# A gated feed-forward layer: gate and up by Strassen's seven block products, and down in eight-bank groups with streamed weights

## The chip, the cores and the metric

The kernel runs on one core of one Trainium2 chip. The metric is the device time of one execution in microseconds (us). The clock named below is the TensorE clock that the profile calls granted. PE is TensorE's matmul side, PEld its weight loads, DVE the vector engine, ACT the scalar engine, POOL the GpSimd engine, SP the sync engine, whose queue ("SPq") issues most DMAs here.

## The reference

```python
# x: 1 x 2048 x 1024, w_gate and w_up: 1024 x 3584, w_down: 3584 x 1024, all bf16
def reference(x, w_gate, w_up, w_down):
    return (gelu_tanh(x @ w_gate) * (x @ w_up)) @ w_down
```

Counted in matmuls of a 128x128 weight block on 512 columns, gate and up are 896 each and down is 896: 2,688 in all.

## The kernel before

The 2,048 tokens are taken in two halves of 1,024, each of two token blocks (`tb`) of 512. For each half: gate and up for all 28 f tiles (tiles of 128 of the 3,584 features), then down. `xT` is x transposed, contraction on the partitions; w_down stays resident in SBUF (`wd_sb`). The very first token block is transposed on PE and copied from PSUM to SBUF by DVE and ACT (such a copy is called an evacuation here); all others come by a transposing DMA.

```python
    def unit(hT, xT_, wg_sb, wu_sb, fi, fc, tb):      # one f tile, one token block
        gate_ps = ps_tile("gate_ps")
        up_ps = ps_tile("up_ps")
        for kd in range(KD):                           # KD = 8
            mm_gu(gate_ps, wg_sb, xT_, fi, tb, kd)     # 128x128 weights, 512 columns
        for kd in range(KD):
            mm_gu(up_ps, wu_sb, xT_, fi, tb, kd)
        unit_tail(hT, gate_ps, up_ps, fc, tb)          # ACT: gelu; DVE: multiply -> hT

    # ... start-up, loads: cut ...
    for h in range(NH):                                # NH = 2
        if h > 0:
            xT = xT_pool.tile([P, KD, SH], BF16, name="xT")
            for tb in range(NTB):                      # two whole transposing loads
                nc.sync.dma_start_transpose(
                    out=xT[:, :, tb * TB : (tb + 1) * TB], in_=xv[t0 : t0 + TB, :, :])
        for fg in range(NFG):
            # ... weights of this group of 4 f tiles: cut ...
            for tb in range(NTB):
                for fi in range(fi_start, FPG):
                    unit(hT, xT, wg_sb, wu_sb, fi, fg * FPG + fi, tb)
        for ts in range(NTS):                          # down: 28 matmuls into one bank
            for dn in range(NDN):
                o_ps = ps_tile("o_ps")
                for fc in range(KF):
                    nc.tensor.matmul(o_ps[:], lhsT=hT[:, fc, ts * P : (ts + 1) * P],
                                     rhs=wd_sb[:, fc, c0 : c0 + DN], ...)
                nc.scalar.copy(out=o_sb[:, c0 : c0 + DN], in_=o_ps[:])
```

Of the kernel before, what the change touches and what calls it, by code (L numbers as in the profile page):

```python
# [11 lines left out]
F32 = mybir.dt.float32  # L12
SCHED_DEP = mybir.DependencyInfo(
    mybir.DependencyClass.NoSync, mybir.DependencyReason.SCHED_ONLY
)


@with_exitstack
def kernel(
# [14 lines left out]
    KD = D // P  # L34
    KF = F // P
    TB = 512
    NH = 2 if S >= 2048 else 1
# [3 lines left out]
    NFG = F // FG  # L41
# [3 lines left out]
    NTS = SH // P  # L45
    TSB = TB // P
    XQ = min(512, D)
    NXQ = D // XQ
    KPQ = XQ // P
    WKP = 2 if KD % 2 == 0 else 1  # L50
    NWP = KD // WKP
    NSU = min(3, FPG)
    NWARM = 9

# [5 lines left out]
    const_pool = ctx.enter_context(tc.tile_pool(name="const", bufs=1))  # L60
    xT_pool = ctx.enter_context(tc.tile_pool(name="xT", bufs=1))
    xs_pool = ctx.enter_context(tc.tile_pool(name="xs", bufs=1))
    hT_pool = ctx.enter_context(tc.tile_pool(name="hT", bufs=1))
    wd_pool = ctx.enter_context(tc.tile_pool(name="wd", bufs=1))
    wgu_pool = ctx.enter_context(tc.tile_pool(name="wgu", bufs=2))
    g_pool = ctx.enter_context(tc.tile_pool(name="g", bufs=3))
    o_pool = ctx.enter_context(tc.tile_pool(name="o", bufs=3))
    psum = ctx.enter_context(
        tc.tile_pool(name="psum", bufs=8, space=bass.MemoryType.PSUM)
    )  # L70

    def ps_tile(name):
        return psum.tile([P, TB], F32, name=name, tag="ps")

    wd_sb = wd_pool.tile([P, KF, D], BF16, name="wd_sb")

    xs0 = xs_pool.tile([P, TSB, D], BF16, name="xs")
    xT = xT_pool.tile([P, KD, SH], BF16, name="xT")
    wg0 = wgu_pool.tile([P, KD, FG], BF16, name="wg_sb")
    wu0 = wgu_pool.tile([P, KD, FG], BF16, name="wu_sb")  # L80
# [7 lines left out]
    def load_w0_piece(wp, eng):  # L88
        k0, k1 = wp * WKP, (wp + 1) * WKP
        eng.dma_start(out=wg0[:, k0:k1, :], in_=wgv[:, k0:k1, 0:FG])  # L90
        eng.dma_start(out=wu0[:, k0:k1, :], in_=wuv[:, k0:k1, 0:FG])

    load_x0_piece(0, nc.sync)
    load_w0_piece(0, nc.scalar)

    nc.scalar.preload_act_table(ACT.Gelu_apprx_tanh)  # L96

# [3 lines left out]
    warm_insts = []  # L101
    if NWARM > 0:
        warm_l = nc.const_aps.tensor(1.0, [P, P], BF16)
        warm_r = nc.const_aps.tensor(1.0, [P, TB], BF16)
        warm_ps = ps_tile("warm_ps")
        for i in range(NWARM):
            warm_insts.append(
                nc.tensor.matmul(  # L108
                    warm_ps[:], lhsT=warm_l, rhs=warm_r, start=True, stop=True
                )  # L110
            )

    x_after = {}
    for q in range(1, NXQ):
        wq = min(max((q * KPQ) // WKP - 1, 0), NWP - 1)
        x_after.setdefault(wq, []).append(q)
    for q in x_after.get(0, []):
        load_x0_piece(q, nc.sync)
    for wp in range(1, NWP):
        load_w0_piece(wp, nc.sync)  # L120
        for q in x_after.get(wp, []):
            load_x0_piece(q, nc.sync)
    for tb in range(1, NTB):
        nc.sync.dma_start_transpose(
            out=xT[:, :, tb * TB : (tb + 1) * TB],
            in_=xv[tb * TB : (tb + 1) * TB, :, :],
        )

    chunk_tiles = {0: (wg0, wu0)}

    def load_chunk(fg):
        wg_sb = wgu_pool.tile([P, KD, FG], BF16, name="wg_sb")
        wu_sb = wgu_pool.tile([P, KD, FG], BF16, name="wu_sb")
        nc.sync.dma_start(out=wg_sb[:], in_=wgv[:, :, fg * FG : (fg + 1) * FG])
        nc.sync.dma_start(out=wu_sb[:], in_=wuv[:, :, fg * FG : (fg + 1) * FG])
        return wg_sb, wu_sb

    if NFG > 1:
        chunk_tiles[1] = load_chunk(1)

    WDP = 4
    for k0 in range(0, KF, WDP):
        k1 = min(KF, k0 + WDP)
        nc.sync.dma_start(out=wd_sb[:, k0:k1, :], in_=wdv[:, k0:k1, :])
# [10 lines left out]
    def transpose_x_piece(q):  # L155
        kds = list(range(q * KPQ, (q + 1) * KPQ))
        banks = []
        if q == 0:
            if TSB % 2 == 0:
                banks.append(([kds[0]], (0, TSB // 2)))  # L160
                banks.append(([kds[0]], (TSB // 2, TSB)))
            else:
                banks.append(([kds[0]], (0, TSB)))
            rest = kds[1:]
            if rest:
                banks.append(([rest[0]], (0, TSB)))
                rest = rest[1:]
        else:
            rest = kds
        for i in range(0, len(rest), 2):  # L170
            banks.append((rest[i : i + 2], (0, TSB)))
        pe_insts = []
        for kd_list, (ts0, ts1) in banks:
            n = (ts1 - ts0) * P
            tp = psum.tile([P, len(kd_list), n], BF16, name="tp", tag="ps")
            for j, kd in enumerate(kd_list):
                for ts in range(ts0, ts1):
                    pe_insts.append(
                        nc.tensor.transpose(  # L179
                            tp[:, j, (ts - ts0) * P : (ts - ts0 + 1) * P],  # L180
                            xs0[:, ts, kd * P : (kd + 1) * P],
                            ident[:],
                        )
                    )
            k0 = kd_list[0]
            evac(xT[:, k0 : k0 + len(kd_list), ts0 * P : ts1 * P], tp[:])
        return pe_insts

    def mm_gu(ps, w_sb, xT_, fi, tb, kd):
        return nc.tensor.matmul(  # L190
            ps[:],
            lhsT=w_sb[:, kd, fi * P : (fi + 1) * P],
            rhs=xT_[:, kd, tb * TB : (tb + 1) * TB],
            start=(kd == 0),
            stop=(kd == KD - 1),
        )

    def unit_tail(hT, gate_ps, up_ps, fc, tb):
        g_sb = g_pool.tile([P, TB], F32, name="g_sb")
        nc.scalar.activation(out=g_sb[:], in_=gate_ps[:], func=ACT.Gelu_apprx_tanh)  # L200
        nc.vector.tensor_tensor(  # L201
            out=hT[:, fc, tb * TB : (tb + 1) * TB],
            in0=g_sb[:],
            in1=up_ps[:],
            op=ALU.mult,
        )

    def unit(hT, xT_, wg_sb, wu_sb, fi, fc, tb):
        gate_ps = ps_tile("gate_ps")
        up_ps = ps_tile("up_ps")  # L210
        for kd in range(KD):
            mm_gu(gate_ps, wg_sb, xT_, fi, tb, kd)
        for kd in range(KD):
            mm_gu(up_ps, wu_sb, xT_, fi, tb, kd)
        unit_tail(hT, gate_ps, up_ps, fc, tb)

    def startup_units(hT, wg_sb, wu_sb):
        groups = [transpose_x_piece(0)]
        su_ps = [(ps_tile("gate_ps"), ps_tile("up_ps")) for _ in range(NSU)]
        for kd in range(KD):  # L220
            for q in range(1, NXQ):
                if kd == q * KPQ - 1:
                    groups.append(transpose_x_piece(q))
            g = [mm_gu(su_ps[u][0], wg_sb, xT, u, 0, kd) for u in range(NSU)]
            g += [mm_gu(su_ps[u][1], wu_sb, xT, u, 0, kd) for u in range(NSU)]
            groups.append(g)
        if warm_insts:
            groups.insert(0, warm_insts)
# [4 lines left out]
        for u in range(NSU):  # L233
            unit_tail(hT, su_ps[u][0], su_ps[u][1], u, 0)

    for h in range(NH):
        if h > 0:
            xT = xT_pool.tile([P, KD, SH], BF16, name="xT")
            for tb in range(NTB):
                t0 = h * SH + tb * TB  # L240
                nc.sync.dma_start_transpose(
                    out=xT[:, :, tb * TB : (tb + 1) * TB],
                    in_=xv[t0 : t0 + TB, :, :],
                )
        hT = hT_pool.tile([P, KF, SH], BF16, name="hT")
        for fg in range(NFG):
            if h == 0 and fg in chunk_tiles:
                wg_sb, wu_sb = chunk_tiles[fg]
            else:
                wg_sb, wu_sb = load_chunk(fg)  # L250
            for tb in range(NTB):
                fi_start = 0
                if h == 0 and fg == 0 and tb == 0:
                    startup_units(hT, wg_sb, wu_sb)
                    fi_start = NSU
                for fi in range(fi_start, FPG):
                    fc = fg * FPG + fi
                    unit(hT, xT, wg_sb, wu_sb, fi, fc, tb)
        for ts in range(NTS):
            last = h == NH - 1 and ts == NTS - 1  # L260
            o_sb = o_pool.tile([P, D], BF16, name="o_sb")
            r0 = h * SH + ts * P
            for dn in range(NDN):
                c0 = dn * DN
                if last and dn == NDN - 1:
                    hh = DN // 2
                    for part in range(2):
                        cc = c0 + part * hh
                        o_ps = ps_tile("o_ps")
# [70 lines left out]
```

## Time and profile before

| before | value | view |
|---|---|---|
| time | 592.9 us, median | executions |
| PE busy | 99% of 590.8 us | page, part 1 |
| longest PE wait | 0.8 us | waits |
| matmul pitch (start to start) | 215.8 ns (768 in 165.76 us) | timeline |
| DVE, ACT, POOL busy | 13%, 15%, 0% | page, part 1 |

Lines of the page of the kernel before: the span, the busy time of each engine (us, share, instructions), the busy share of PE and the granted TensorE clock in 40 slices (9 is 90% or more), and the chain of work that ended last by engine.

```profile
span 590.8 us, 6172 instructions
...
PE 586.4 (99%) x2757; PEld 268.6 (45%) x2757; DVE 78.7 (13%) x116; ACT 88.9 (15%) x148; POOL 0.7 (0%) x6
...
PE   8999999999999999999999999999999999999997
...
PEclk9999999999999999999999999999999999999999
...
PE 99%; DMA 1%; ACT 0%; issue 0%
```

Groups of instructions by shape, kernel before. The columns are line, engine, operation, output<-inputs, shapes, count; then busy us, mean ns of one; then idle time just before them.

```profile
L190 PE MATMUL gate_ps<-xT,wg_sb 128*128 128x512 bf16 x896 | 212.5, 379 | 0.0
L295 PE MATMUL o_ps<-wd_sb,hT 128*128 128x512 bf16 x868 | 187.7, 379 | 0.0
L190 PEld LDWEIGHTS <-wg_sb 128*128 128x128 bf16 x896 | 87.6, 98 | 105.2
```

Timeline rows of the kernel before around the second half of the start, and at the change of half (start us, duration us, engine, line, operation, count, idle time before).

```profile
7.19 6.64 SPq L124 DMA_TRANSPOSE xT<-in_x_dram  x1
11.11 0.69 DVE L150 COPY xT<-tp 128x1024 bf16<-128x1024 bf16 x1 [4.56 <-PE tp L179]
12.65 0.81 PE L190 MATMUL gate_ps<-xT,wg_sb 128*128 128x512 bf16 x3
...
201.09 10.59 SPq L241 DMA_TRANSPOSE xT<-in_x_dram  x2
```

How to read this: PE never stops, so only fewer or cheaper matmuls can help. The 379 ns of a matmul is its latency; they overlap, and one starts every 215.8 ns (eight take 1.73 us from row to row of the timeline). The weight load, 98 ns, hides behind the matmul before it. The last fence shows two things that the change touches: DVE evacuates the second PE-transposed piece of x at 11.1 us, in time for the matmul at 12.65 us, and the two whole transposing loads at the change of half keep the SP queue busy for 10.6 us, when it has nothing urgent to issue.

### The profile page before, as it was taken

How to read it: one execution, taken by the hardware profiler on the slowest of the kernel's cores; microseconds unless marked ns; L12 is line 12 of the kernel's file. 1: busy time of each engine (PE TensorE's matmuls, PEld its weight loads, DVE VectorE, ACT ScalarE, POOL GpSimd, SP SyncE). 2: the span in 40 equal slices, each digit the busy share in tenths (PEclk: the TensorE clock that was granted, in tenths of full speed). 3: DMA queues.
4: the chain of work that ended last, by engine and by line, in shares of the span. 5: the costliest groups of instructions: out<-in, count | busy, mean ns of one | idle time of the engine just before them, and what ended most of it. 6: DMA issues, size and time to landing. Idle time of an engine off the chain costs nothing.

```text
span 590.8 us, 6172 instructions
## 1 busy us (share of the span) xinstructions
PE 586.4 (99%) x2757; PEld 268.6 (45%) x2757; DVE 78.7 (13%) x116; ACT 88.9 (15%) x148; POOL 0.7 (0%) x6
## 2 busy tenths in 40 slices
PE   8999999999999999999999999999999999999997
PEld 4444444444444444444444444444444444444445
DVE  0211211121122100000011221121122110000000
ACT  2211112111111110101011112111111110101010
POOL 0000000000000000000000000000000000000000
PEclk9999999999999999999999999999999999999999
DMA  9991404041231480000000413214040000000001
GB/s 273 358 378 59 143 0 143 8 136 52 92 99 44 127 176 19 24 31 18 19 18 3 140 41 103 85 58 131 12 143 1 0 1 0 24 30 19 18 19 36
DMA packets 48969, 45.47 MB, mean 77 GB/s; under 512 B 13360, under 2 KB 43440, under 8 KB 48944
## 3 DMA queue, kind: packets, MB, share of 16 engines
q1 hardware_dynamic: 45952, 40.44, 22.0%
q10 hardware_dynamic: 2992, 4.65, 2.2%
q8 instruction: 21, 0.34, 0.2%
q14 instruction: 4, 0.03, 0.0%
HBM read 37.75 MB, written 4.19 MB: 71 GB/s over the span
## 4 chain that ended last, share of the span: by engine, by line
PE 99%; DMA 1%; ACT 0%; issue 0%
PE up_ps L190 33%; PE gate_ps L190 33%; PE o_ps L295 32%; PE o_ps L271 1%; DMA xs<-in_x_dram 1%; PE tp L179 0%; ACT o_sb L287 0%
## 5 line engine op out<-in xcount | busy, mean ns | idle before, releaser
L190 PE MATMUL up_ps<-xT,wu_sb 128*128 128x512 bf16 x896 | 212.5, 379 | 0.0
L190 PE MATMUL gate_ps<-xT,wg_sb 128*128 128x512 bf16 x896 | 212.5, 379 | 0.0
L295 PE MATMUL o_ps<-wd_sb,hT 128*128 128x512 bf16 x868 | 187.7, 379 | 0.0
L190 PEld LDWEIGHTS <-wu_sb 128*128 128x128 bf16 x896 | 87.6, 98 | 106.0 <-DMA wu_sb<-in_w_up_dram 0.5
L190 PEld LDWEIGHTS <-wg_sb 128*128 128x128 bf16 x896 | 87.6, 98 | 105.2
L295 PEld LDWEIGHTS <-hT 128*128 128x128 bf16 x868 | 84.9, 98 | 102.4
L201 DVE TENSOR_TENSOR hT<-g_sb,up_ps 128x512 bf16<-128x512 f32 x112 | 76.9, 688 | 403.2 <-PE up_ps L190 403.2
L200 ACT ACTIVATE g_sb<-gate_ps 128x512 f32<-128x512 f32 x112 | 66.7, 597 | 312.4 <-PE gate_ps L190 312.4
L302 ACT CAST o_sb<-o_ps 128x512 bf16<-128x512 f32 x31 | 18.2, 586 | 172.6 <-PE o_ps L295 172.6
L279 DVE CAST o_sb<-o_ps 128x256 bf16<-128x256 f32 x1 | 0.4, 425 | 93.0 <-PE o_ps L271 93.0
L271 PE MATMUL o_ps<-wd_sb,hT 128*128 128x256 bf16 x56 | 6.3, 273 | 0.0
L271 PEld LDWEIGHTS <-hT 128*128 128x128 bf16 x56 | 5.5, 98 | 0.9
L108 PE MATMUL warm_ps<-const-bfloat16-1.0 128*128 128x512 bf16 x9 | 4.0, 629 | 0.8 <-PEq L324 0.8
L152 ACT COPY xT<-tp 128x1024 bf16<-128x1024 bf16 (+1 forms) x3 | 2.4, 799 | 7.1 <-PE tp L179 7.1
L179 PE MATMUL tp<-ident,xs 128*128 128x128 bf16 x32 | 2.1, 219 | 0.7 <-DMA xs<-in_x_dram 0.7
L150 DVE COPY xT<-tp 128x256 bf16<-128x256 bf16 (+2 forms) x3 | 1.4, 469 | 10.4 <-PE tp L179 10.4
L179 PEld LDWEIGHTS <-xs 128*128 128x128 bf16 x32 | 1.9, 98 | 1.8 <-DMA xs<-in_x_dram 1.6
L108 PEld LDWEIGHTS <-const-bfloat16-1.0 128*128 128x128 bf16 x9 | 1.2, 141 | 2.7 <-issue 2.7
L96 ACT ACT_TABLE_LOAD x1 | 1.3, 1283 | 1.8 <-issue 1.8
L287 ACT CAST o_sb<-o_ps 128x256 bf16<-128x256 f32 x1 | 0.4, 372 | 5.5 <-PE o_ps L271 5.5
masks.py:199 POOL TENSOR_SCALAR_AFFINE_SELECT ident<-ident 128x128 bf16<-128x128 bf16 x1 | 0.3, 294 | 0.1
masks.py:197 POOL MEMSET ident<- 128x128 bf16 x1 | 0.2, 205 | 0.3 <-POOLq L324 0.3
(4 smaller groups left out, 0.4 us busy)
## 6 DMA issues: line engine op xcount, KB each, us to landing
wg_sb<-in_w_gate_dram SPq DMA_DIRECT2D x13, 1024.0 KB, 5.2
wu_sb<-in_w_up_dram SPq DMA_DIRECT2D x13, 1024.0 KB, 6.8
wd_sb<-in_w_down_dram SPq DMA_DIRECT2D x7, 1024.0 KB, 13.8
out_dram<-o_sb ACTq DMA_DIRECT2D x15, 256.0 KB, 2.0
xs<-in_x_dram SPq DMA_DIRECT2D x2, 512.0 KB, 5.9
wg_sb<-in_w_gate_dram SPq DMA_DIRECT2D x3, 256.0 KB, 6.5
wu_sb<-in_w_up_dram SPq DMA_DIRECT2D x3, 256.0 KB, 6.8
wg_sb<-in_w_gate_dram ACTq DMA_DIRECT2D x1, 256.0 KB, 4.4
```

Source lines behind the costliest of these rows:

```text
L96: nc.scalar.preload_act_table(ACT.Gelu_apprx_tanh)
L108: nc.tensor.matmul(warm_ps[:], lhsT=warm_l, rhs=warm_r, start=True, stop=True)
L150: nc.vector.tensor_copy(out=dst, in_=src)
L152: nc.scalar.copy(out=dst, in_=src)
L179: nc.tensor.transpose(tp[:, j, (ts - ts0) * P : (ts - ts0 + 1) * P], xs0[:, ts, kd * P : (kd + 1) * P], ident[:],)
L190: return nc.tensor.matmul(ps[:], lhsT=w_sb[:, kd, fi * P : (fi + 1) * P], rhs=xT_[:, kd, tb * TB : (tb + 1) * TB], start=(kd == 0), stop=( ...
L200: nc.scalar.activation(out=g_sb[:], in_=gate_ps[:], func=ACT.Gelu_apprx_tanh)
L201: nc.vector.tensor_tensor(out=hT[:, fc, tb * TB : (tb + 1) * TB], in0=g_sb[:], in1=up_ps[:], op=ALU.mult,)
L271: nc.tensor.matmul(o_ps[:, 0:hh], lhsT=hT[:, fc, ts * P : (ts + 1) * P], rhs=wd_sb[:, fc, cc : cc + hh], start=(fc == 0), stop=(fc == KF - 1),
L279: nc.vector.tensor_copy(out=o_sb[:, cc : cc + hh], in_=o_ps[:, 0:hh])
L295: nc.tensor.matmul(o_ps[:], lhsT=hT[:, fc, ts * P : (ts + 1) * P], rhs=wd_sb[:, fc, c0 : c0 + DN], start=(fc == 0), stop=(fc == KF - 1),)
L302: nc.scalar.copy(out=o_sb[:, c0 : c0 + DN], in_=o_ps[:])
```

## The change: intent and diff

A pair of f tiles and the two token blocks, with the contraction split in two halves, form a 2x2 by 2x2 block product. Done plainly, it takes 8 block products of 4 matmuls for gate and 8 for up: 64. The Winograd form of Strassen's scheme needs 7 each: 56. The price is sums of blocks. Sums of weight blocks (s1 to s4) are made on POOL one pair ahead, sums of x blocks (t1 to t4) once per half on DVE and POOL, and sums of products by accumulating in PSUM, seeding a bank with an ACT copy of another, and DVE additions. So as not to round the sums to bf16, they are stored as float32r (a 32-bit type that this kernel's matmuls take as operands), and so are their partners (a22, b22): in this kernel the two operands of a matmul always have the same type. The sums need SBUF, so w_down is no longer resident: 512 KB pieces are streamed through three buffers, for groups of 8 PSUM banks.

The core of the diff, cut (the first four f tiles of the first half keep the old form):

```diff
+    def t_sums(eng4):                       # per half; b(j, l): half j of contraction, block l
+        tt(out=tsum["t1"][:], in0=b(0, 1), in1=b(0, 0), op=sub)                 # DVE
+        tt(out=tsum["t2"][:], in0=b(1, 1), in1=tsum["t1"][:].bitcast(F32), op=sub)
+        nc.scalar.copy(out=tsum["b22"][:], in_=b(1, 1))                         # ACT
+        tt(out=tsum["t3"][:], in0=b(1, 1), in1=b(0, 1), op=sub)
+        eng4.tensor_tensor(out=tsum["t4"][:], ...)                              # POOL
...
+    def pair_quads(hT, h, pair, nxt):       # j: gate, up; PB, VB, QB, RB: two banks each
+        for j in range(2):
+            mm(PB[j], j, block(key, j, 0, 0), b11, True)                        # bf16
+            nc.scalar.copy(out=banks[QB[j]][:], in_=banks[PB[j]][:])            # seed
+        for j in range(2):
+            mm(VB[j], j, s(j, "s1"), tsum["t1"], True)                          # float32r
+            nc.scalar.copy(out=m5[j][:], in_=banks[VB[j]][:])
+            prep(j, "s1")                   # POOL: the same sum for the next pair
+        for j in range(2):
+            mm(QB[j], j, s(j, "s2"), tsum["t2"], False)                         # float32r
+            nc.scalar.copy(out=banks[RB[j]][:], in_=banks[QB[j]][:])
+            nc.vector.tensor_tensor(out=banks[QB[j]][:], ... m5[j] ..., op=ALU.add)
...          # P block (bf16), then s3 x t3, s4 x b22, a22 x t4 (float32r), gelu and multiply
...
-    for ts in range(NTS):                   # down, w_down resident
+            for kk in range(NKK):           # 14 pieces of two f tiles, w_down streamed
+                while len(wd_tiles) < n + 3:
+                    load_wd(len(wd_tiles))  # 512 KB, three buffers, on the SP queue
+                if fillers:
+                    fillers.pop(0)()        # one of 16 small transposing x loads, ...
+                for b in range(8):
+                    for c in range(WDT): nc.tensor.matmul(banks[b][...], ...)
```

## The prediction

> **What bounds the kernel now.** PE does. The page has PE 99% busy, the chain that ended last is 99% PE (gate 33%, up 33%, down 32%), and the waits list no PE wait above 0.8 us. The granted clock is 1.000. The stage windows give 372 matmuls in 80 us of a warm stage, 215 ns each (I use 215.5; the groups' 379 ns is latency). Weight loads last 98 ns and hide behind the matmul before them. DVE (13%), ACT (15%) and POOL (0%) can take work.
>
> **What the change does.**
> - It replaces 64 matmuls by 56 in each of 26 pairs: 208 fewer. 208 x 0.2155 = 44.8 us off the critical path.
> - Of the 56, 40 have float32r operands: 1,040 matmuls whose weight load is no longer an instruction of its own in the compiled order. No trace here shows what such a matmul costs. "TensorE: Matmul & The Clock Gate" (Weight-path perf modes) says that fast weight load is off for FP32, which would lengthen the load. I assume that it streams a row at bf16's rate and that its load still hides: 0 us. Every 43 ns more per matmul eats the whole gain.
> - A pair's PE time is 56 x 0.2155 = 12.1 us. ACT gets 12 instructions of about 0.6 us (gelu 597 ns) = 7.2 us; DVE 8 of 688 ns = 5.5 us; POOL 8 sums of 128x512. From the 4,497 ns at 2,048 elements in "GPSIMD Engine Reference" (section 3.1) I estimate 1.1 to 1.3 us each, 9 to 10 us: POOL is the fullest, but each sum is asked for one pair ahead. The order of quads leaves 2 us or more for each PSUM copy. I expect no PE wait within a pair.
> - Startup: the compiled order puts t1 on DVE (and b22 on ACT) ahead of the evacuation of the second PE-transposed x piece, and t1 waits for the transposed x load, issued at 7.2 us with 10.3 us to landing: 17.5 us. t1 (2,048 elements into float32) then needs about 2.3 us and the evacuation 0.7. PE, which needed that evacuation at 12.6 us, gets it near 20.5: 8 us of PE idle. Then the clock falls to half ("TensorE: Matmul & The Clock Gate", Part 1): 1.7 us more. Together +10 us.
> - Change of half: 16 small transposed loads stand before the fourth wd load in the SP queue (two whole ones took 10.6 us of issue before), so streamed wd may come late: +2 us (0 to 6). Elsewhere a 512 KB wd piece per 3.45 us is 152 GB/s, under the 350 to 390 GB/s that the early slices show.
>
> **Sum.** 592.9 - 44.8 + 10 + 2 + 0.5 = 560.6. Predicted 561 us, 550 to 600. Chances: faster by over 2% 0.74, within 2% 0.06, slower by over 2% 0.20.
>
> **What would show each step.** Matmul pitch in a window inside the pairs: 215 ns says float32r is free. About 2,550 PE matmuls instead of 2,757. Waits: one PE wait of about 8 us on DVE (evacuation) near 12 to 20 us, with a low clock slice after it; few or no PE waits on POOL or ACT; at most a few us of PE on wd_sb in mid-kernel. POOL near 40% busy over the span, sums 1.1 to 1.3 us.
>
> **What would make it wrong.** A float32r matmul that streams at half rate (+224 us), or whose weight load is exposed (about 100 ns each, +104 us); POOL sums above 1.5 us, which make POOL the bound of a pair.

## The result, and the profile after

| | before | after |
|---|---|---|
| median | 592.93 us | 583.1 us (581.59 to 583.31) |
| ratio after/before | | 0.9821 (0.9802 to 0.9841) |
| PE waits over 1.5 us | none | 9.0 us on wd_sb, 5.6 us on xT |

The ratio is not quite the ratio of the medians. Both kernels gave correct results. The change won 9.8 us where about 32 had been forecast.

The same lines of the page after:

```profile
span 581.5 us, 6767 instructions
...
PE 559.9 (96%) x2523; PEld 336.3 (58%) x2523; DVE 176.2 (30%) x241; ACT 200.5 (34%) x343; POOL 248.8 (43%) x216
...
PE   7799999999999939999999999999999999999997
...
PEclk9799999999999969999999999999999999999999
...
PE 91%; DMA 4%; SPq 3%; DVE 0%; ACT 0%; issue 0%; ACTq 0%; DVEq 0%
```

PE has two holes that it did not have, in slices 1 and 2 and in slice 15 (the row "PE"), and the clock row falls in slices 2 and 15. The chain is no longer PE alone: 3% of it is the SP queue.

Groups after, same columns:

```profile
L298 PE MATMUL bank<-t,s 128*128 128x512 f32 x624 | 161.0, 406 | 0.0
L298 PE MATMUL bank<-xT,wu_sb 128*128 128x512 bf16 x208 | 53.4, 379 | 0.0
L298 PEld LDWEIGHTS bank<-t,s 128*128 128x128 f32 x624 | 117.4, 188 | 29.0
L277 POOL TENSOR_TENSOR s<-wg_sb 128x512 fp32r<-128x512 bf16 x26 | 31.8, 1224 | 175.6 <-PE bank L298 157.6
```

The weight load of a float32r matmul takes 188 ns instead of 98. POOL's sums take 1.17 to 1.25 us, as estimated, and no PE wait inside a pair shows up. One pair on PE, in the timeline after (its first float32r row merges two products; the first float32r matmul after bf16 ones lasts 578 ns in the trace, 189 more than the others, so its row starts early and the bf16 row before it looks short):

```profile
107.12 1.04 PE L298 MATMUL bank<-xT,wg_sb 128*128 128x512 bf16 x4
107.99 1.03 PE L298 MATMUL bank<-xT,wu_sb 128*128 128x512 bf16 x4
108.67 4.00 PE L298 MATMUL bank<-t,s 128*128 128x512 f32 x16
112.51 1.04 PE L298 MATMUL bank<-xT,wg_sb 128*128 128x512 bf16 x4
113.38 1.03 PE L298 MATMUL bank<-xT,wu_sb 128*128 128x512 bf16 x4
114.06 2.19 PE L298 MATMUL bank<-t,s 128*128 128x512 f32 x8
116.09 1.98 PE L298 MATMUL bank<-b,s 128*128 128x512 f32 x8
117.90 1.97 PE L298 MATMUL bank<-t,a 128*128 128x512 f32 x8
119.72 1.04 PE L298 MATMUL bank<-xT,wg_sb 128*128 128x512 bf16 x4
```

The pair takes 119.72 - 107.12 = 12.60 us; 56 matmuls at 215.8 ns would be 12.08. The eight of the last product take 119.72 - 117.90 = 1.82 us, 227 ns each, while four bf16 ones take 0.87 us, 216 to 218 ns each.

The two holes, in the chain of waits after, in order of time (start us, duration us, what). Left out are the first pairs and, of the sixteen loads "SPq L122" from 190.94 us on, all but two; the others are alike (the first one is cut short by the chain).

```profile
7.61 8.11 DMA xT<-in_x_dram
...
15.85 2.29 DVE t L252
18.14 0.61 DVE xT L185
18.75 0.04 issue
18.79 25.33 PE bank L153 x104
...
205.57 1.26 SPq L122
...
209.48 1.26 SPq L122
...
210.85 3.94 DMA wd_sb<-in_w_down_dram
214.78 0.04 issue
214.83 38.00 PE bank L399 x166
```

Start: the transposing x load ends at 15.7 us, DVE then makes t1, and only then evacuates the second PE-transposed piece, which PE has waited for since 13.2 us. Change of half: the sixteen small transposing loads (L122) occupy the SP queue until 210.8 us; the fourth w_down piece is issued only then, and PE, done with the first three pieces near 205.8 us, starts again at 214.83.

Stage by stage, from the first matmul of each stage in the two traces:

| stage | before, us | after, us | difference | forecast |
|---|---|---|---|---|
| start, to the first f tile that the change rewrites | 35.10 | 43.96 | +8.86 | +10 |
| gate and up, first half (12 pairs) | 165.76 | 151.36 | -14.40 | -20.7 |
| down, first half, with the change of half | 96.69 | 108.73 | +12.04 | +2 |
| gate and up, second half (14 pairs) | 193.39 | 176.39 | -17.00 | -24.1 |
| down, second half, and the end | 99.90 | 101.08 | +1.18 | +0.5 |
| span | 590.84 | 581.52 | -9.32 | |

The forecast of the pairs is 12 and 14 times 8 x 0.2155 us. So two terms were mis-sized: the pairs gave 13.4 us less than they should have, and the change of half cost 10 us more.

### The profile page after: what moved, and what is told of

Its sections match the earlier page's. It is cut to its first block, busy times and chain, and to the rows that moved or that the text cites. A ratio compares the mean times of both kernels' runs of the same rounds, so it can differ in the third digit from the quotient of the medians.

```text
span 581.5 us, 6767 instructions
## 1 busy us (share of the span) xinstructions
PE 559.9 (96%) x2523; PEld 336.3 (58%) x2523; DVE 176.2 (30%) x241; ACT 200.5 (34%) x343; POOL 248.8 (43%) x216
## 4 chain that ended last, share of the span: by engine, by line
PE 91%; DMA 4%; SPq 3%; DVE 0%; ACT 0%; issue 0%; ACTq 0%; DVEq 0%
PE bank L298 56%; PE bank L399 31%; PE bank L153 4%; SPq L122 3%; DMA xT<-in_x_dram 1%; DMA out_dram<-o_sb 1%; DMA wu_sb<-in_w_up_dram 1%; DMA wd_sb<-in_w_down_dram 1%; DVE t L252 0%; ACT o_sb L411 0%; DVE xT L185 0%; ACTq L112 0%; ACT o_sb L427 0%; ACTq L411 0%; DVEq L252 0%
## 5 line engine op out<-in xcount | busy, mean ns | idle before, releaser
L399 PE MATMUL bank<-wd_sb,hT 128*128 128x512 bf16 x898 | 196.1, 381 | 9.7 <-DMA wd_sb<-in_w_down_dram 9.0
L298 PE MATMUL bank<-t,s 128*128 128x512 f32 x624 | 161.0, 406 | 0.0
L399 PEld LDWEIGHTS <-hT 128*128 128x128 bf16 x898 | 88.2, 98 | 117.3 <-issue 13.5
L298 PEld LDWEIGHTS bank<-t,s 128*128 128x128 f32 x624 | 117.4, 188 | 29.0
L277 POOL TENSOR_TENSOR s<-wg_sb 128x512 fp32r<-128x512 bf16 x26 | 31.8, 1224 | 175.6 <-PE bank L298 157.6
L167 DVE TENSOR_TENSOR hT<-g_sb,bank 128x512 bf16<-128x512 f32 x112 | 76.9, 688 | 75.0 <-ACT g_sb L163 31.1
L163 ACT ACTIVATE g_sb<-bank 128x512 f32<-128x512 f32 x112 | 66.6, 596 | 88.7 <-DVE bank L341 49.9
L329 DVE TENSOR_TENSOR bank<-bank,m 128x512 f32<-128x512 f32 x52 | 36.4, 700 | 113.3 <-ACT bank L328 111.5
L435 DVE CAST o_sb<-bank 128x512 bf16<-128x512 f32 x15 | 10.4, 692 | 174.5 <-PE bank L399 170.3
L298 PE MATMUL bank<-xT,wg_sb 128*128 128x512 bf16 x208 | 53.9, 382 | 0.0
L282 POOL TENSOR_TENSOR s<-wg_sb 128x512 fp32r<-128x512 bf16 x26 | 32.4, 1247 | 21.7 <-PE bank L298 21.7
L341 DVE TENSOR_TENSOR bank<-bank,m 128x512 f32<-128x512 f32 x52 | 36.4, 700 | 9.9 <-PE bank L298 9.9
L328 ACT COPY bank<-bank 128x512 f32<-128x512 f32 x52 | 29.7, 571 | 17.0 <-PE bank L298 17.0
L298 PEld LDWEIGHTS <-wu_sb 128*128 128x128 bf16 x208 | 20.3, 98 | 24.7 <-issue 0.3
L320 ACT COPY bank<-bank 128x512 f32<-128x512 f32 x52 | 29.6, 571 | 13.4 <-PE bank L298 13.4
```

The source lines that it names most:

```text
L163: nc.scalar.activation(out=g_sb[:], in_=ps[:], func=ACT.Gelu_apprx_tanh)
L167: nc.vector.tensor_tensor(out=hT[:, fc, tb * TB : (tb + 1) * TB], in0=g_sb[:], in1=ps[:], op=ALU.mult,)
L277: tt(out=t[:], in0=a(1, 0), in1=a(1, 1), op=ALU.add)
L282: tt(out=t[:], in0=a(0, 0), in1=a(1, 0), op=ALU.subtract)
L298: nc.tensor.matmul(banks[bank][:], lhsT=lhs[:, c, :], rhs=rhs[:, c, :], start=start and c == 0, stop=c == KH - 1, skip_group_check=True,)
L320: nc.scalar.copy(out=banks[QB[j]][:], in_=banks[PB[j]][:])
```

## The experiments

Each kernel is the changed one with one edit, or several where the table says so; all gave correct results. Times are medians; the kernel before ran beside them at 592.9 to 593.0 us (one of its executions, at 2,131 us and a clock of 0.275, is left out).

| run | edit | us | ratio to before (95%) |
|---|---|---|---|
| changed kernel | | 583.1 | 0.9821 (0.9802 to 0.9841) |
| e1_sums_later | x sums after the first units | 579.6 | 0.9765 (0.974 to 0.979) |
| e5_startup_all | and the a22 copies too | 576.0 | 0.9709 (0.9691 to 0.9727) |
| e2_wd_first | w_down loads ahead of x loads | 574.9 | 0.9679 (0.9648 to 0.9711) |
| e3_whole_transposes | two whole x loads | 571.3 | 0.9619 (0.9594 to 0.9644) |
| e4_half_columns | float32r matmuls in two halves | 593.8 (one run) | |
| e6_both | e5 and e3 together | 564.1 | 0.9508 (0.9486 to 0.953) |
| e8_both_obuf | e6 and a fourth output buffer | 563.9 | 0.9502 (0.9486 to 0.9518) |
| e7_both_bf16 | e6 with bf16 sums | 550.6 | 0.9284 (0.9265 to 0.9304) |

### The start: order on DVE and ACT

Theory: DVE and ACT run their queues in order, and the scheduler put t1 and b22, which wait for a late load, ahead of an evacuation that PE needs early. Rival: the loads themselves hold PE. The edit adds ordering hints only (cut):

```diff
-            t_sums(nc.gpsimd)
+            t1_inst, t3_inst, b22_inst = t_sums(nc.gpsimd)
+            for a, b in ((t1_inst, last_mult), (t3_inst, last_mult), (b22_inst, last_gelu)):
+                tc.add_manual_dep(a.ins, b.ins.name, SCHED_DEP, reason="sums after units")
```

> Only the issue order changes: t1, t3 (DVE) and b22 (ACT) are held behind the first three units' gelu and mult, so that the second x piece is evacuated first. Theory (order on the in-order DVE and ACT queues makes PE wait 5.6 us at 13 to 19 us of the trace, and the halved clock after it costs the rest): no PE wait on an xT evacuation, clock 1.00 in the early slices, first Strassen pair starts near 35 us instead of 44.0 us, total 583.1 - 8.9 = about 574 us. Rival (the load traffic at the start or the x transposes themselves hold PE, not the order): the pair still starts later than 40 us and the total stays above 579 us.

Measured: 579.6 us; the wait on the evacuation is gone, as the theory has it, but the first pair starts at 38.7 us, between the two forecasts, and the total is above 579 us, as the rival has it. So this run alone does not decide. Part of what the start won was lost later: the wait on wd_sb grew from 9.0 to 10.1 us. The timeline names the rest of the start: ACT now stood still for the a22 copies, which wait for the second group's weights, and the first gelu stood behind them; PE waited for that gelu. Rows of the timeline of this run:

```profile
23.69 0.62 ACT L293 CAST a<-wu_sb 128x512 fp32r<-128x512 bf16 x1 [3.81 <-DMA wu_sb<-in_w_up_dram]
24.22 1.56 ACT L165 ACTIVATE g_sb<-bank 128x512 f32<-128x512 f32 x3
...
24.86 1.89 PE L153 MATMUL bank<-xT,wg_sb 128*128 128x512 bf16 x7 [1.88 <-ACT g_sb L165]
```

The same fault a second time, hidden until then under the first. The next edit holds the a22 copies back as well:

```diff
-                    s_sum(0, first_pair, j, name)
+                    inst = s_sum(0, first_pair, j, name)
+                    if name == "a22":
+                        tc.add_manual_dep(inst.ins, last_gelu.ins.name, SCHED_DEP, ...)
```

> The start alone mended in full, the change of half left as it was: t1, t3, b22 and the a22 copies behind the first three units. The run with the later sums alone won 3.5 us of the 8.9 that the trace puts on the start; there PE waited 1.9 us for the first gelu, which stood on ACT behind the a22 copies and their weight loads. Theory (that wait and the clock's phase at the start make up the difference): no such wait, first pair at 35 to 37 us, total 574 to 576 us. Rival (the start is worth only about 3.5 us in truth): 579 us or more.

Measured: 576.0 us, at the edge of the theory's range, and no PE wait in the start over 1.1 us. The first pair of the profiled execution starts at 37.26 us, just past the 35 to 37 expected and 2.2 us later than in the kernel before; its first transposes and matmuls ran at the slow clock until about 10 us, which differs between executions (this one took 577.4 us, the other three 575.8 to 576.1; the profiled one with both faults mended started its first pair at 35.69). The order is the cause; 7.1 of the 8.9 us are won back alone, while the wait on wd_sb grew by 0.7 us, to 9.7.

### The change of half: issue time or bandwidth

Theory A: the SP queue was busy issuing. Theory B: too many bytes at once. Two edits, each against B in another way. The first leaves the sixteen small loads and puts each behind a w_down load:

```diff
+                        tr = load_xT(xT, nh, tb, kd, kd + 1)
+                        tc.add_manual_dep(tr.ins, last_wd[0].ins.name, SCHED_DEP, reason="wd first")
```

> Only the order on the SP queue changes: each of the 16 small transposed x loads of the change of half is issued behind the wd load of its step. Theory A (the fourth wd piece was late because 16 transposed loads of about 1.25 us of issue time each stood before it on SP): the PE wait of 9.0 us on wd_sb goes, the clock stays 1.00, total about 583.1 - 11 = 572 us. Theory B (DMA bandwidth: streamed wd, weights and transposed x together are too much for that stage): PE still waits on wd_sb or on later xT users, in total 5 us or more, and the total stays above 577 us.

Measured: 574.9 us, between the two numbers. The wait on wd_sb is gone, as A has it. PE waits 1.3 and 1.1 us later, at a change of bank groups, on the output evacuations. The trace names both: ACT's (247.44 us) had waited 3.9 us for a store to free its output tile, and DVE's (249.23) stood behind t1 (247.02 to 249.31), which had waited for an x load that now came late. The granted clock then fell to half from about 250.2 to 253.6 us. No run isolates these.

The second keeps x ahead of w_down but in two loads instead of sixteen:

```diff
-                for kd in range(KD):
-                    fillers.append(lambda tb=tb, kd=kd: load_xT(xT, nh, tb, kd, kd + 1))
+                fillers.append(lambda tb=tb: load_xT(xT, nh, tb, 0, KD))
+                fillers += [lambda: None] * (KD - 1)
```

> The same bytes of x, but two whole transposed loads in place of 16 small ones, still ahead of the wd load on SP. Theory A (SP issue time): two whole loads took 10.6 us of SP in the kernel before, so SP is free for the fourth wd piece near 201 us of the trace instead of 210.9, and the PE wait of 9.0 us falls to 0 to 2 us; total about 572 to 574 us. Theory B (bandwidth): the transposed bytes are as many and move at the same time, so the wait stays at 5 us or more.

Measured: 571.3 us. The SP queue of this run:

```profile
190.03 10.40 SPq L122 DMA_TRANSPOSE xT<-in_x_dram  x2
200.49 0.57 SPq L372 DMA_DIRECT2D wd_sb<-in_w_down_dram  x1
```

and of the changed kernel:

```profile
190.04 20.70 SPq L122 DMA_TRANSPOSE xT<-in_x_dram  x16
210.85 0.52 SPq L372 DMA_DIRECT2D wd_sb<-in_w_down_dram  x1
```

The same bytes took 10.40 us of issue instead of 20.70, the fourth w_down piece left 10.4 us earlier, and PE had no wait on wd_sb; the wait at the start (5.5 us) stayed, as it should. Down of the first half took 97.77 us instead of 108.73. Bandwidth is ruled out: in the 20 us after the start of down this run moved 270 GB/s, and nothing was late.

### The float32r matmul

A float32r matmul starts 227 ns after the one before it, a bf16 one 216 ns. The load of 188 ns starts when the matmul before starts, and the next matmul follows about 38 ns after its end, which looks like a bound by the load. Theory A says so; theory B puts the difference down to the stream or to a fixed cost. The edit halves the columns:

```diff
+            w = TB // 2 if lhs.dtype == F32R else TB
+            for q0 in range(0, TB, w):
+                for c in range(KH):
+                    nc.tensor.matmul(banks[bank][:, q0 : q0 + w], lhsT=lhs[:, c, :],
+                                     rhs=rhs[:, c, q0 : q0 + w], ...)
```

> Every float32r matmul of 512 columns becomes two of 256 with the same weights: 80 instead of 40 in a pair, same arithmetic. Theory A (the float32r pitch of 227 ns is its own weight load, 188 ns plus about 38 ns that cannot overlap the load, so it does not depend on columns): each half still takes about 227 ns, a pair takes about 16 x 216 + 80 x 227 = 21.6 us instead of 12.6, and the total rises by about 26 x 9 = 235 us, to about 815 us. Theory B (float32r streams a little slower than bf16, or has a fixed 11 ns per matmul): each half takes 114 to 125 ns, a pair takes 12.6 to 13.4 us, and the total rises by 0 to 22 us.

Measured: 593.8 us (one run). The end of one pair and the next, on PE:

```profile
106.33 2.08 PE L300 MATMUL bank<-t,a 128*128 128x256 f32 x16
108.25 1.04 PE L300 MATMUL bank<-xT,wg_sb 128*128 128x512 bf16 x3
...
119.39 2.08 PE L300 MATMUL bank<-t,a 128*128 128x256 f32 x16
121.31 1.04 PE L300 MATMUL bank<-xT,wg_sb 128*128 128x512 bf16 x3
```

Sixteen halves take 108.25 - 106.33 = 1.92 us: 120 ns each, not 227. Theory A is refuted: loads that last 191 ns each follow one another every 120 ns, so they overlap. From 256 to 512 columns the pitch grows by 227 - 120 = 107 ns for 256 columns, 0.418 ns a column; bf16 in the kernel before grows by 215.8 - 109.2 = 106.6 ns between its 256-column matmuls (56 in 6.28 us at the end; without the last one's latency of 0.273 us, 55 pitches of 109.2 ns) and the others. So the columns cost the same, and float32r has a fixed surcharge of about 11 ns per matmul, at 256 columns (120 - 109.2) as at 512 (227 - 215.8). The pair agrees with a cost per instruction: it grows from 12.60 to 121.31 - 108.25 = 13.06 us for 40 more matmuls without one more column, 11.5 ns for each. What in the instruction makes that surcharge stays open: every float32r matmul of these kernels has its own load, so no run separates the two.

### Both faults mended, and the surcharge taken away

> Both order faults mended: whole transposed x loads at the change of half, and at the start t1, t3, b22 and also the two a22 copies (which held the first gelu back in the run with the later sums alone) behind the first three units. The account of the lost time says: 583.1 - 8.9 (start) - 11 (change of half, wait and slow clock) = about 563 us, no PE wait over 1.5 us, granted clock 1.00 outside the first 5 us, first pair starting near 35 us. If the two losses hide other work, the gains don't add and the total stays above 567 us.

Measured: 564.1 us. The edits add up: e5 won 7.1 us and e3 11.8, together 18.9, and this run 19.0. The PE waits of this run:

```profile
PE bank L209 <- DMA xs<-in_x_dram: 0.8, 1, 0.8
PE bank L141 <- PEq L520: 0.8, 1, 0.8
PE bank L405 <- ACT o_sb L417: 0.7, 1, 0.7
PE bank L405 <- DMA wd_sb<-in_w_down_dram: 0.4, 1, 0.4
```

(Columns: who waited for whom, us in total, times, the longest; two waits of 0.2 us are left out.) Next, all sums in bf16 on top of that, which rounds the sums and is less exact on purpose:

```diff
-            tsum[name] = t_pool.tile([P, KH, TB], F32R, name=name)
+            tsum[name] = t_pool.tile([P, KH, TB], BF16, name=name)
-        t = s_pool.tile([P, KH, P], F32R, name=f"{name}_{j}")
+        t = s_pool.tile([P, KH, P], BF16, name=f"{name}_{j}")
```

> As the kernel with both faults mended, but all block sums in bf16, so every matmul is a bf16 one; less exact on purpose, it may or may not pass the comparison. Theory (float32r costs a fixed 11 ns per matmul, and nothing else in a pair makes PE wait): a pair takes 56 x 0.216 = 12.1 us instead of 12.6, 26 pairs save 13 to 14 us, total about 549 us. Rival (the seeded PSUM accumulation, its copies or the POOL sums pace a pair): a pair stays at 12.4 us or more and the saving is under 6 us.

Measured: 550.6 us, and the result still passed the comparison with the reference; by how much, the run does not say. The end of a pair and the next:

```profile
108.13 1.89 PE L304 MATMUL bank<-t,a 128*128 128x512 bf16 x8
109.86 1.03 PE L304 MATMUL bank<-xT,wg_sb 128*128 128x512 bf16 x4
...
120.22 1.67 PE L304 MATMUL bank<-t,a 128*128 128x512 bf16 x7
121.94 1.03 PE L304 MATMUL bank<-xT,wg_sb 128*128 128x512 bf16 x4
```

The pair takes 121.94 - 109.86 = 12.08 us, which is 56 matmuls at bf16's pitch. So neither the seeded accumulation nor the copies nor POOL paces a pair: the 0.52 us of the changed kernel is float32r alone, 13 ns for each of the 40 matmuls, 13.5 us over 26 pairs (564.1 - 550.6 gives the same). That is about 2 ns more than the pitches above give within a run of float32r matmuls; the rest must fall where the types change, which no run isolates.

A smaller question, the fourth output buffer:

> As the kernel with both faults mended, plus a fourth output tile buffer. Theory: with three, the fourth output tile of each 8-bank group waits for the first tile's store to land (ACT idle 3.5 us on it in mid-kernel, 1.0 us at the end), which costs PE 0.9 us at a group change and the tail about 1 us: about 2 us less than the kernel with three. Rival: the tail is set by the last stores alone, no gain (within 0.5 us).

Measured: 563.9 us against 564.1: no gain, the rival holds. The ACT wait for the store does go, but the last stores set the end. In this run the last matmul ends at 558.3 us of a span of 562.2, 3.9 us before the end; with three buffers (`e6_both`) it was 4.4 (558.4 of 562.8), so half a microsecond of the tail went, less than the theory's one.

## Why the prediction was wrong

- **What bounds the kernel (PE alone): right.** When both holes were closed, time followed the matmul count and pitch again.
- **208 matmuls fewer, 44.8 us: right.** The bf16 version has pairs of 12.08 us; its span is 550.4 us, 40.4 less than before, and a later start (+2), waits and the end make up the difference.
- **The float32r step failed.** "I assume that it streams a row at bf16's rate and that its load still hides: 0 us" was right about the row and roughly right about the load, but not about the zero: there is a surcharge per matmul, which measured 13 ns, 13.4 us over 1,040 matmuls. The text gave 43 ns as the break-even and weighed only zero, 100 ns and double; nobody asked what a few per cent of a pitch are worth when it occurs a thousand times. "TensorE: Matmul & The Clock Gate" of the Trainium skill (Weight-path perf modes) says that fast weight load is off for FP32; it does not name float32r, and the trace agrees as far as that the load lasts 188 ns instead of 98. But the load is not what paces PE: half-size matmuls of 120 ns follow each other with loads of 191 ns.
- **The change of half failed, and it is the other half of the miss.** "Streamed wd may come late: +2 us (0 to 6)" became +12.0: 9.0 us of PE wait, about 2.0 us of slow clock after it (the granted clock was at half until 218.9 us, 4.1 us of matmuls at half speed; 108.73 - 97.77 - 9.0 gives the same), the rest at the change of bank groups. The right queue and the right collision were named, but sixteen small transposing loads were taken to cost in sum what two whole ones had cost (10.6 us); they took 20.7, about 1.26 us each against 5.2 on average for eight times the size.
- **The start: right, its size partly by luck.** Forecast +10 us, measured +8.86: the wait was 5.6 us instead of 8, mainly because the x load ended at 15.7 us instead of 17.5; the clock cost more than the 1.7 us forecast: the 24 matmuls from 18.79 to 26.69 us took 7.90 us where 24 x 0.2158 = 5.18. The two errors partly cancel. The same order fault on ACT (the a22 copies, found by `e1_sums_later`) was not foreseen. The clock agrees with "TensorE: Matmul & The Clock Gate" of the skill (Part 1), which has it at half after an idle window: the granted clock of the profile is 0.50 between 20 and 24 us.
- **POOL: right.** From a figure of "GPSIMD Engine Reference" (3.1) of the skill the prediction estimated 1.1 to 1.3 us for a sum; the trace has 1.17 to 1.25, POOL is 43% busy, and no pair waits for it.

In sum: 13.4 us from float32r and 10.0 us from the change of half, less 1.1 us at the start and 0.7 us more at the end, is 23.0 us, against 22.1 us between 561 and 583.1 (the rest is the rounding of 560.6 to 561 and spans of one profiled execution set against medians).

## What to carry to other kernels

When a change gives TensorE fewer but other matmuls, multiply even a few ns of pitch by their number before calling them free. When loads or sums are added, read the compiled order of every in-order queue and ask of each entry that waits for a late load what stands behind it: here that cost 8.9 us on DVE and ACT and 11 us on SP (108.73 - 97.77), nearly half of the 44.8 us of matmuls saved, and ordering hints and larger loads brought 19 us back with the arithmetic untouched. After mending one such order, look again: a second fault may be hidden under the first.

## What the Trainium skill lacked or had wrong

- "TensorE: Matmul & The Clock Gate" has no rate for float32r matmuls. Here: 227 ns at 512 columns and 120 ns at 256, against 215.8 and 109.2 for bf16; a load of 188 to 191 ns against 98.
- The same page (Part 2, Back-to-back issue gap) gives a sustained 131 ns per 512-column matmul for streams of load and matmul and says that its formula of 216 ns over-counts there. Here such streams of bf16 run at 215.8 ns in the kernel before and 12.08 us for 56 in `e7_both_bf16`; the formula fits, the 131 ns do not.
- "DMA: Bandwidth & Descriptors" does not say how the time for which a transposing load holds the queue that issues it depends on its size; its only figure before trn3 is one in cycles, for small tiles. Here: about 1.26 us for 128 KB (x 128 wide, 512 tokens) and 5.2 us on average for 1 MB, so that sixteen small ones hold it for 20.7 us and two whole ones for 10.4.
- "TensorE: Matmul & The Clock Gate" (Part 1) says that what is issued in the first 3.4 us or so runs at half clock and everything after it at full clock. Here matmuls ran at half clock for about 5.6 us after the wait of 5.6 us (18.79 to 24.35 us) and for about 4.1 us after that of 9.0 us (214.83 to 218.9). The granted clock was at half from 17.5 to 24.35 and from 208.6 to 218.9 us, 6.8 and 10.3 us, close to two and three times 3.4: that fits the free-running window of the same part, but the budget of 3.4 us was too small both times.
